# Pooled attention and a chosen expert: choosing the expert, loading its weights, the first tiles' keys and the rows set aside, rearranged

## The chip, the cores and the metric

The kernel runs on one core of one Trainium2 chip. The number that counts is the device time of one execution in microseconds (us). The engines have short names here: PE multiplies matrices, DVE works on vectors, ACT applies functions, POOL is GpSimd, SP only issues transfers (DMAs). Each engine runs its own list of instructions strictly in order and waits where an input isn't there yet.

## The reference

```python
kv_pool = kv.reshape(B, H // 4, 4, W // 4, 4, C).mean(axis=(2, 4))
k = v = kv_pool.reshape(B, -1, C) @ w_sr              # 768 keys a batch
a = softmax(q @ k.T / sqrt(C));  x = (a @ v).reshape(B * S, D)
logits = x @ w_gate;  expert_idx = argmax(logits)      # 8 experts
out[row] = softmax(logits)[expert] * (relu(x[row] @ w1[expert]) @ w2[expert])
```

There are 4 batches of 12288 queries with 128 channels, 768 pooled keys for each batch, 8 experts with 1024 hidden features. All is float32.

## The kernel before

The queries are cut into 96 tiles of 512 rows, 24 to a batch (`SPB`). A tile goes through attention (scores of 768 keys, maximum, exponential, transposes, values), the gate's logits, the routing, and the expert's two layers. Each float32 product is made of three matmuls on a high and a low part of the operands (`mm3`, lines 221 to 223): `kh`/`kl`, `qh`/`ql`, `pth`/`pt`, `xh`/`xl`, `hh`/`hlow`, `wt`. ACT makes the high parts (line 215), DVE or POOL the low ones (lines 218 and 909).

In a batch nearly all rows choose the same expert. `pick` finds it from the first tile of a batch: it marks each row's expert (`oh`, line 533), adds the marks (`tot`), lets PE sum them over the 128 partitions (line 546), and takes the largest. SP reads its number into a register and loads the two weight matrices (`load_weights`); `cut` splits them into a high part (ACT) and a low part (POOL, 4 pieces). The first layer is `first()`, the second `second()`; every tile is computed with its batch's expert.

Rows with another expert are strangers. When a chunk of tiles has been routed (three chunks in a batch: tiles 0 to 8, 9 to 16, 17 to 23), `collect` ranks its strangers (`xoh`, `bt`, `xtot`, a sum on PE in lines 637 and 638, then `pos` on POOL and `place`) and `put_row` (line 689) writes them with one indirect DMA of POOL for each 128 rows into `lists`, 4 units of time apart. The last batch's rows are put only at the end of the program and only if need be. Two extra tiles (`EXTRA`), inserted in the last batch, take 128 rows of `lists` each (line 1008, `xid`), gather their queries and compute them. After the last tile DVE counts what is left (`more`, lines 1201 to 1207); every engine loads `more` (line 1208) and, if it is not zero, runs a loop over the rest. In the run shown it is zero.

The keys of a batch are averaged on DVE (`raw`, line 264), turned on PE, projected (line 306) and split. For batch 0 this happens at the start; for the others during the batch before. The first three tiles (`FIRST`) transpose their exponentials on PE (line 808), and write them in the keys' interleaved order; all later ones transpose on DVE and DMA.

The order on each engine follows from a plan: a heap of (time, function). `AT` is a table of offsets for a tile's steps in units (16 units to a tile, one tile takes about 20 us). `plan.at` places a step, `series` a chain of steps that waits for a free bank of PSUM. What is popped first is emitted first, and engines run it in that order. Three PSUM banks are handed round with `take` and `give`.

Of the kernel before, what the change touches and what calls it, by code (L numbers as in the profile page):

```python
# [30 lines left out]
    "turn_q": -17.69, "high_q": -9.56, "low_q": -7.35, "maxima": 1.36, "exps": 1.9, ("scores", 0): 0.0,  # L31
    ("scores", 1): 3.8, ("scores", 2): 8.16, ("scores", 3): 12.21, ("first_p", 0): 8.67, ("first_p", 1): 5.16,
    ("first_p", 2): 4.44, ("first_p", 3): 8.51, ("first_p", 4): 5.05, ("first_p", 5): 5.87, "first_high": 0.8,
    "first_low": 1.23, "first_values": 2.54, "turn_p": 3.06, "move_p": 17.26, ("high_p", 0): 23.35,
    ("high_p", 1): 26.36, ("high_p", 2): 28.89, "low_p": 6.59, ("values", 0): 34.89, ("values", 1): 37.47,
    ("values", 2): 37.48, ("values", 3): 40.72, ("values", 4): 45.71, ("values", 5): 46.95, "high_x": 0.7,
    "low_x": 1.18, "logits": 3.5, "diag": 4.81, "route": 6.37, "step": 0.4, "scale_exp": 2.53, "scale": 3.11,
    "apart": 5.66, "spread": 7.89, "keep_s": 8.68, ("first", 0): 66.38, ("first", 1): 67.88,
    ("first", 2): 68.9, ("first", 3): 70.58, ("first", 4): 73.63, ("first", 5): 74.3, ("first", 6): 76.79,
    ("first", 7): 78.4, "high_h": 0.57, "low_h": 1.51, "second": 5.06, "turn_y": 0.94, "scale_y": 2.2,  # L40
    "put": 9.84, "early_q": -13.19, "cut": -3.88, "cut_step": 1.05,
# [39 lines left out]
def tile_pooled_attention_top1_moe(ctx: ExitStack, tc, q, kv, w_sr, w_gate, w1, w2, out):  # L81
# [68 lines left out]
    eidx = iota("eidx", [[1, E]], 0, 0)  # L150
    order_l = iota("order_l", [[-1, NL]], NL, 0)
# [91 lines left out]

    def keys(t, b, step):
# [66 lines left out]
        def high_kv(kb):  # L311
            pr, ks = own["pr", kb], slice(kb * P, (kb + 1) * P)
            nc.scalar.mul(out=own["kh"][:, ks], in_=pr[:, :P], mul=scale)
            high(own["vh"][:, kb], pr[:, P : P + C])

        def low_kv(kb):
# [13 lines left out]
        for kb in range(NB):  # L330
# [17 lines left out]
    def load_weights(own):  # L348
        for n in range(2):
            own[n] = kp.tile([P, POOL // 2, POOL * C], F32, name="raw", bufs=3)  # L350
        nc.sync.dma_start(
            out=own[0].rearrange("p r c -> p (r c)"),
            in_=w1[bass.ds(own["ex"], 1)].rearrange("o p f -> p (o f)"),
        )
        nc.sync.dma_start(
            out=own[1].rearrange("p r (f d) -> p (r f) d", d=D),
            in_=w2[bass.ds(own["ex"], 1)].rearrange("o (f p) d -> p (o f) d", p=P),
        )
# [18 lines left out]
    chunks = [range(0, 9), range(9, 17), range(17, SPB)]  # L377
# [15 lines left out]
    def route(t, i, own):  # L393
# [44 lines left out]
        def firsts():  # L438
# [4 lines left out]
            )  # L443

# [150 lines left out]
    def collect(t, b, c):  # L595
# [88 lines left out]
        if b < B - 1:  # L684
            steps += [(4.0 if n else 1.0, put_row, b, c, n) for n in range(A)]
# [556 lines left out]
```

## Time and profile before

| | us |
|---|---|
| median of 3 runs | 2071.72 (2071.35 to 2072.4) |
| profiled execution | 2071.68 |
| its span in the profile | 2070.0 |
| PE busy | 2008.7 (97%) |
| DVE busy | 1605.3 (78%) |
| ACT busy | 1323.6 (64%) |
| POOL busy | 1317.9 (64%) |

The span is the time from the first to the last event of the profile, and 1.7 us of the execution lie outside it. A busy share is an average over the whole span. A wait is told by the engine that waited, what ended it, and how long the engine had been idle. The start of an operation and its length stand in the timeline; when two operations overlap in an engine's pipeline, their lengths add up to slightly more than the time they take.

### The profile page before, as it was taken

The numbers are of one execution on the slowest core, as the hardware profiler recorded it, in microseconds if no ns is written. First come the engines' busy times: TensorE is split into PE (matmuls) and PEld (weight loads), VectorE is DVE, ScalarE is ACT, GpSimd is POOL, SyncE is SP. The second block draws the span as 40 slices with busy tenths as digits, with TensorE's granted clock in tenths as the row PEclk, the third lists the DMA queues.
The fourth block names the chain that finished last, engine by engine and source line by source line (L and its number), as shares of the span: only waits on it lengthen the run. The fifth ranks groups of instructions, "written<-read, shape, count | busy, mean of one in ns | idle before, by whom it ended". The sixth has DMA issues, their size and how long they took to land.

```text
span 2070.0 us, 29923 instructions
## 1 busy us (share of the span) xinstructions
PE 2008.7 (97%) x9358; PEld 1657.5 (80%) x9358; DVE 1605.3 (78%) x2646; ACT 1323.6 (64%) x2630; POOL 1317.9 (64%) x1163
## 2 busy tenths in 40 slices
PE   6899999999999999999999999999999999999997
PEld 5688888878878888878878888887887888887885
DVE  5677779987777788997787777998777777777764
ACT  3666666666666666666666666666666666666663
POOL 1154576687687666777778657668678765545441
PEclk9899999999999999999999999999999999999998
DMA  6455556655565455756456545665646454646431
GB/s 172 74 122 114 105 100 147 149 122 115 113 131 119 96 119 107 151 124 141 95 126 129 118 91 119 129 146 126 127 91 131 92 119 95 161 83 143 97 77 22
DMA packets 497652, 239.91 MB, mean 116 GB/s; under 512 B 427440, under 2 KB 433714, under 8 KB 497488
## 3 DMA queue, kind: packets, MB, share of 16 engines
q1 hardware_dynamic: 488144, 237.69, 54.8%
q0 software_dynamic: 9344, 0.26, 0.3%
q8 instruction: 75, 1.23, 0.2%
q14 instruction: 89, 0.73, 0.1%
HBM read 59.97 MB, written 31.92 MB: 44 GB/s over the span
## 4 chain that ended last, share of the span: by engine, by line
PE 87%; DVE 6%; DMA 2%; SPq 1%; issue 1%; ACT 1%; POOL 1%; DVEq 0%; POOLq 0%; ACTq 0%
PE ps L221 28%; PE ps L223 28%; PE ps L222 28%; DVE hlow L909 1%; DVE nmax L751 1%; PE ps L403 1%; PE ps L402 1%; DVE pb L778 1%; SPq L788 1%; ACT prob L768 1%; DVE half L264 1%; PE ps L306 0%; PE ps L808 0%; SPq L258 0%; DMA pt<-pb 0%
## 5 line engine op out<-in xcount | busy, mean ns | idle before, releaser
L909 DVE SCALAR_TENSOR_TENSOR hlow<-ps,hh 128x512 fp32r<-128x512 f32 x768 | 520.1, 678 | 225.7 <-ACT hh L905 214.7
L218 POOL TENSOR_TENSOR pt<-pt,pth 128x1024 fp32r<-128x1024 f32 x279 | 672.9, 2415 | 34.0 <-ACT pth L215 26.8
L905 ACT ACTIVATE hh<-ps 128x512 fp32r<-128x512 f32 x768 | 458.6, 597 | 328.4 <-PE ps L223 224.5
L768 ACT ACTIVATE prob<-ps,nmax 128x768 f32<-128x768 f32 x384 | 354.4, 923 | 272.6 <-DVE nmax L751 259.4
L778 DVE STREAM_TRANSPOSE pb<-prob 128x768 f32<-128x768 f32 x372 | 359.0, 965 | 107.0 <-ACT prob L768 104.8
L751 DVE TENSOR_REDUCE nmax<-ps 128x1 f32<-128x768 f32 x384 | 363.5, 947 | 57.3 <-PE ps L223 49.5
L689 POOL DMA_INDIRECT lists<-row,dst x288 | 289.2, 1004 | 60.6 <-issue 54.8
L221 PE MATMUL ps<-hh,wt 128*128 128x512 f32 x768 | 312.0, 406 | 0.0
L221 PE MATMUL ps<-xh,wt 128*128 128x512 f32 x768 | 306.5, 399 | 2.7 <-ACT wt L215 2.5
L223 PE MATMUL ps<-xl,wt 128*128 128x512 f32 x768 | 305.5, 398 | 0.0
L222 PE MATMUL ps<-xh,wt 128*128 128x512 f32 x768 | 304.2, 396 | 0.6 <-POOL wt L218 0.6
L222 PE MATMUL ps<-hh,wt 128*128 128x512 f32 x768 | 303.2, 395 | 0.0
L223 PE MATMUL ps<-hlow,wt 128*128 128x512 f32 x768 | 303.1, 395 | 0.0
L215 ACT CAST pth<-pt 128x1024 fp32r<-128x1024 f32 x279 | 291.8, 1046 | 16.0 <-DMA pt<-pb 14.6
L221 PE MATMUL ps<-kh,qh 128*128 128x256 f32 (+2 forms) x768 | 260.9, 340 | 3.3 <-ACT prob L768 3.1
L223 PE MATMUL ps<-kl,qh 128*128 128x256 f32 (+2 forms) x768 | 260.1, 339 | 0.0
L222 PE MATMUL ps<-kh,ql 128*128 128x256 f32 (+2 forms) x768 | 260.0, 339 | 0.0
L937 POOL TENSOR_TENSOR yo<-yb,sb 128x512 f32<-128x512 f32 x96 | 101.0, 1052 | 221.6 <-issue 109.3
L223 PE MATMUL ps<-pt,vh 128*128 128x512 f32 x558 | 220.7, 396 | 0.0
L221 PE MATMUL ps<-pth,vh 128*128 128x512 f32 x558 | 220.6, 395 | 0.0
L222 PE MATMUL ps<-pth,vl 128*128 128x512 f32 x558 | 218.5, 392 | 0.0
L218 POOL TENSOR_TENSOR ql<-qt,qh 128x512 fp32r<-128x512 f32 x96 | 125.0, 1302 | 117.1 <-ACT qh L215 62.2
(212 smaller groups left out, 2987.5 us busy)
## 6 DMA issues: line engine op xcount, KB each, us to landing
pt<-pb SPq DMA_DIRECT2D x372, 384.0 KB
qb<-in_q_dram SPq DMA_DIRECT2D x384, 64.0 KB
out_dram<-yo SPq DMA_DIRECT2D x384, 64.0 KB
raw<-in_kv_dram SPq DMA_DIRECT2D x84, 256.0 KB
raw<-in_moe_w_dram SPq DMA_DIRECT2D x12, 512.0 KB
lists<-row,dst POOLq DMA_INDIRECT x288, 2.3
pth<-in_kv_dram SPq DMA_DIRECT2D x12, 256.0 KB
kvs<-kh SPq DMA_DIRECT2D x4, 384.0 KB
```

The costliest lines, as they stand in the source:

```text
L215: nc.scalar.copy(out=dst, in_=src)
L218: eng.tensor_tensor(out=dst, in0=src, in1=h.bitcast(F32), op=ALU.subtract)
L221: nc.tensor.matmul(out=ps, lhsT=wh, rhs=xh, start=start, stop=False)
L222: nc.tensor.matmul(out=ps, lhsT=wl, rhs=xh, start=False, stop=False)
L223: nc.tensor.matmul(out=ps, lhsT=wh, rhs=xl, start=False, stop=stop)
L689: put = nc.gpsimd.indirect_dma_start(out=lists, out_offset=bass.IndirectOffsetOnAxis(ap=state["dst", b, c][:, n : n + 1].bitcast(U32), axi ...
L751: nc.vector.tensor_reduce(out=nmax, in_=own["s", a], op=ALU.max, axis=AX.XY if i < HEAD else AX.X, negate=True)
L768: nc.scalar.activation(out=p_out, in_=s_in, func=AF.Exp, bias=own["nmax", a], scale=1.0, accum_out=grp["sums"][:, k : k + 1],)
L778: nc.vector.transpose(out=own["pb"][:, :, :, a, :].rearrange("p c b t -> p b c t"), in_=own["prob", a].rearrange("p (b c t) -> p b c t", c ...
L905: nc.scalar.activation(out=hh, in_=own["hp", f], func=AF.Relu)
L909: nc.vector.scalar_tensor_tensor(out=hl, in0=own["hp", f], scalar=0.0, in1=own["hh", f].bitcast(F32), op0=ALU.max, op1=ALU.subtract,)
L937: nc.gpsimd.tensor_tensor(out=own["yo"], in0=own["yb"].rearrange("p (n d) -> p n d", d=SQ), in1=sb.unsqueeze(2).broadcast_to([P, G * G, SQ ...
```

## The change

`pick` loses `oh`: the routing's own marks `sc` (8 for expert 0 down to 1) are added at once, and the sums weighed with `even`. Weights come in four DMAs, two for each matrix, and `first()` and `second()` wait each for their own piece. The chunks become four (0 to 8, 9 to 16, 17 to 20, 21 to 23). In the last batch the rows of the first three chunks are put during the batch, 2 units apart, and `more` is made in the last chunk's `collect`. The first three tiles write their exponentials contiguously: batch 0's keys are in natural order for them, with own value tiles `v_first` (in the spare weight buffer), and a second projection makes the interleaved values (`values_project`). The last tile is computed in two halves of 256 columns, turned and scaled by DVE, and written from two queues. The extra tiles wait for a free bank, and their `turn_q` comes later. The table `AT` has new numbers.

```diff
-    "put": 9.84, "early_q": -13.19, "cut": -3.88, "cut_step": 1.05,
+    "second": 5.06, "turn_y": 0.58, "scale_y": 2.2, "put": 9.84, "early_q": -13.17, ("cut", 0): -3.88,
+    ("cut", 1): -0.27, ("cut", 2): 0.9, ("cut", 3): 1.28, "values_first": 0.3, "extra": -0.18,
+    "extra_q": 14.55, "count": 0.96, "ranks": 0.61,
...
+    v_first = [wts[1][:, n, : NB * C].rearrange("p (n c) -> p n c", c=C) for n in range(2)]
...
+        def mean_first(kb):
+            own["pTn", kb] = kp.tile([P, P], F32, name="pooled")
+            nc.scalar.mul(out=own["pTn", kb], in_=own["pt", kb][:, :P], mul=1.0 / (POOL * POOL))
+            give(own["pt", kb])
+            own["pT", kb] = kp.tile([P, P], F32, name="pooledT")
+            nc.gpsimd.tensor_copy(out=by_key(own["pT", kb]), in_=split_keys(own["pTn", kb]))
...
+            if b == 0:
+                nc.tensor.matmul(out=pr[:, :P], lhsT=wsr_sb, rhs=own["pTn", kb], start=True, stop=True)
+                nc.tensor.matmul(out=pr[:, P : P + C], lhsT=own["pTn", kb], rhs=wsr_sb, start=True, stop=True)
+                return
...
+        @takes_bank
+        def values_project(kb):
+            own["pv", kb] = take()
+            nc.tensor.matmul(out=own["pv", kb][:, :C], lhsT=own["pT", kb], rhs=wsr_sb, start=True, stop=True)
...
-        nc.sync.dma_start(
-            out=own[0].rearrange("p r c -> p (r c)"),
-            in_=w1[bass.ds(own["ex"], 1)].rearrange("o p f -> p (o f)"),
-        )
...
+        for c in range(F // T):
+            cs = slice(c * T, (c + 1) * T)
+            nc.sync.dma_start(
+                out=own[0][:, c], in_=w1[bass.ds(own["ex"], 1), :, cs].rearrange("o p f -> p (o f)")
+            )
...
-    chunks = [range(0, 9), range(9, 17), range(17, SPB)]
+    chunks = [range(0, 9), range(9, 17), range(17, 21), range(21, SPB)]
...
-        def onehot():
-            after("first", b, 0)
-            own["oh"] = rp.tile([P, G, E], F32, name="oh")
...
+                nc.vector.reduce_sum(
+                    out=own["tot"], in_=state["group", b, 0]["sc"].rearrange("p g e -> p e g"), axis=AX.X
+                )
...
+            own["av"] = own["ct"][:, E : 2 * E]
+            nc.vector.tensor_tensor(out=own["av"], in0=own["ct"][:, :E], in1=even, op=ALU.mult)
...
+            if b == B - 1:
+                steps += [(0.1, counts, n) for n in range(3)]
+        if b < B - 1 or c < len(chunks) - 1:
+            step = 4.0 if b < B - 1 else 2.0
+            steps += [(step if n else 1.0, put_row, b, c, n) for n in range(A)]
...
-            if i < FIRST:
-                p_out = by_key(prob).rearrange("p (h n) c t -> p h n c t", h=2)
-                s_in = s_in.rearrange("p h (n c t) -> p h n c t", t=SQ, c=P // SQ)
-            elif i < HEAD:
+            if i < HEAD:
                 p_out = prob.rearrange("p (h k) -> p h k", h=2)
...
-            for n in range(2):
-                for c in range(F // T):
-                    after("cut", b, n, c)
+            after("cut", b, 0, f * P // T)
...
+        def last_y(h):
...
+            nc.vector.transpose(out=own["yb"][:, hs], in_=own["y"][h])
+            nc.vector.tensor_tensor(
+                out=own["yo"][:, ts], in0=own["yb"][:, hs].rearrange("p (n d) -> p n d", d=SQ),
...
+                (nc.sync if k % P < 2 * SQ else nc.scalar).dma_start(
...
-        t += 8.0
+        t += AT["extra_q"]
...
-    go = nc.values_load(more[0:1, 0:1], min_val=0, max_val=NTOK // P + NL)
+    go = nc.values_load(state["more"][0:1, 0:1], min_val=0, max_val=NTOK // P + NL)
     with tc.If(go > 0):
-        for c, tiles in enumerate(chunks):
-            for n in range(len(tiles) * G):
-                put_row(B - 1, c, n)
+        for n in range(len(chunks[-1]) * G):
+            put_row(B - 1, len(chunks) - 1, n)
```

On POOL, where the second batch begins, the program before runs these steps from the end of the first batch's last `collect` (`left`) to the first low part of the second batch's weights (`wt_78`); `lists` are the puts.

```order
L674 TENSOR_TENSOR left<-rows,start 128x8
L937 TENSOR_TENSOR yo<-yb,sb 128x512
L689 DMA lists<-row,dst 397312x2 x2
L459 TENSOR_TENSOR dn<-df,rinv 128x32
L218 TENSOR_TENSOR ql<-qt,qh 128x512
L689 DMA lists<-row,dst 397312x2 x2
L218 TENSOR_TENSOR pt<-pt,pth 128x4x256
L486 TENSOR_TENSOR sx<-row,quad 128x16
L689 DMA lists<-row,dst 397312x2
L218 TENSOR_TENSOR wt_78<-raw,wt_78 128x512
```

After the change the same stretch of POOL reads:

```order
L710 TENSOR_TENSOR left<-rows,start 128x8
L1004 TENSOR_TENSOR yo<-yb,sb 128x512
L743 DMA lists<-row,dst 397312x2 x3
L502 TENSOR_TENSOR dn<-df,rinv 128x32
L226 TENSOR_TENSOR ql<-qt,qh 128x512
L743 DMA lists<-row,dst 397312x2 x3
L226 TENSOR_TENSOR pt<-pt,pth 128x4x256
L529 TENSOR_TENSOR sx<-row,quad 128x16
L743 DMA lists<-row,dst 397312x2 x2
L226 TENSOR_TENSOR wt_78<-raw,wt_78 128x512
```

Eight puts stand there in place of five; in the whole stretch from the `dn` two tiles earlier there are 22 in place of 12.

On DVE, at the ranks of the second chunk's strangers, the program before has these steps up to `xtot`, the operand of PE's sum:

```order
L712 STREAM_TRANSPOSE qt<-qb 128x4x4x32
L778 STREAM_TRANSPOSE pb<-prob 128x6x4x32
L625 TENSOR_REDUCE bt<-xoh 128x64
L909 SCALAR_TENSOR_TENSOR hlow<-ps,hh 128x512
L632 TENSOR_REDUCE xtot<-bt 128x8
L218 TENSOR_TENSOR xl<-ps,xh 128x512
```

After the change they read:

```order
L962 SCALAR_TENSOR_TENSOR hlow<-ps,hh 128x512
L829 STREAM_TRANSPOSE pb<-prob 128x6x4x32
L661 TENSOR_REDUCE bt<-xoh 128x64
L668 TENSOR_REDUCE xtot<-bt 128x8
L962 SCALAR_TENSOR_TENSOR hlow<-ps,hh 128x512
L226 TENSOR_TENSOR xl<-ps,xh 128x512
```

One `hlow` that stood ahead of `xtot` stands behind it.

On DVE at the end of the program before, `more` is the last thing that is made:

```order
L665 TENSOR_REDUCE place<-pos 128x28
L909 SCALAR_TENSOR_TENSOR hlow<-ps,hh 128x512 x7
L932 STREAM_TRANSPOSE yb<-ps 128x512
L1201 TENSOR_SCALAR cnt<-left 128x32
L1202 TENSOR_SCALAR cnt<-cnt 128x32
L1207 TENSOR_REDUCE more<-cnt 128x1
```

After the change the end of DVE's list reads:

```order
L701 TENSOR_REDUCE place<-pos 128x12
L718 TENSOR_SCALAR cnt<-left 128x32
L720 TENSOR_SCALAR cnt<-cnt 128x32
L727 TENSOR_REDUCE more<-cnt 128x1
L962 SCALAR_TENSOR_TENSOR hlow<-ps,hh 128x512 x7
L1015 STREAM_TRANSPOSE yb<-ps 128x256
L1016 TENSOR_TENSOR yo<-yb,sb 128x256
L1015 STREAM_TRANSPOSE yb<-ps 128x256
L1016 TENSOR_TENSOR yo<-yb,sb 128x256
```

The three steps that make `more` have moved ahead of seven `hlow` and of the last tile's result, and the last product stands on DVE.

## Rows read from the trace of the kernel before

**Rows 1.** The page, busy time of the engines: us (share of the span) xinstructions.

```profile
PE 2008.7 (97%) x9358; PEld 1657.5 (80%) x9358; DVE 1605.3 (78%) x2646; ACT 1323.6 (64%) x2630; POOL 1317.9 (64%) x1163
```

**Rows 2.** The waits of PE over the whole span. A line of the program that waited, what it waited for: us in total, times, longest us.

```profile
PE ps L546 <- DVE tot L541: 7.0, 3, 2.4
PE ps L637 <- DVE xtot L632: 6.2, 4, 1.9
PE ps L808 <- ACT prob L768: 5.6, 4, 2.4
...
PE ps L221 <- ACT prob L768: 3.1, 4, 1.8
...
PE ps L1034 <- DVE hlow L909: 1.7, 1, 1.7
...
PE ps L1034 <- DMA half<-in_q_dram,xidn: 1.3, 1, 1.3
```

**Rows 3.** The end of the program. First the timeline (start us, us, engine line op out<-in, idle time before it and what ended it), then what lines 1208, 1209 and 1238 issued there (engine's queue, operation, times, shortest/median/longest ns, first and last start in us).

```profile
2047.13 0.20 POOL L674 TENSOR_TENSOR left<-rows,start 128x8 f32<-128x8 f32 x1
...
2054.88 0.40 PE L223 MATMUL ps<-hlow,wt 128*128 128x512 f32 x1
...
2055.38 0.72 DVE L932 STREAM_TRANSPOSE yb<-ps 128x512 f32<-128x512 f32 x1 [1.07 <-PE ps L223]
...
2056.23 1.05 POOL L937 TENSOR_TENSOR yo<-yb,sb 128x512 f32<-128x512 f32 x1 [7.89 <-issue]
...
2057.31 2.75 SPq L946 DMA_DIRECT2D out_dram<-yo  x4
...
L1208 POOLq TENSOR_LOAD <-more x1: 513/513/513, 2056.6 to 2056.6; - x1
...
L1209 POOLq EVENT_SEMAPHORE  x5: 17/43/43, 2060.2 to 2060.6; - x5
...
L1209 POOLq INC_SWDGE_SEM  x1: 1795/1795/1795, 2060.7 to 2060.7; - x1
...
L1238 POOLq DRAIN  x3: 40/107/6615, 2062.5 to 2069.7; - x3
...
L1238 SPq DRAIN  x3: 7/7/13, 2063.2 to 2069.4; - x3
```

**Rows 4.** The timeline of ACT, an exponential of the first tile and one of the fourth.

```profile
36.69 1.60 ACT L768 ACTIVATE prob<-ps,nmax 128x768 f32<-128x768 f32 x1 [2.02 <-DVE nmax L751]
...
90.45 0.90 ACT L768 ACTIVATE prob<-ps,nmax 128x768 f32<-128x768 f32 x1 [1.68 <-DVE nmax L751]
```

**Rows 5.** What line 306 issued: the projection of the pooled keys on PE, shortest/median/longest ns, first and last start.

```profile
L306 PE MATMUL ps<-pooledT,wsr_sb x48: 386/406/582, 13.3 to 1435.0; 128*128 128x128 f32 x48
```

**Rows 6.** One stretch of the span: from:to, length, busy us (instructions) of PE, PE's weight loads, DVE, ACT and POOL, granted clock of PE as a share of full speed, DMA share, GB/s.

```profile
50.00:100.00 50.00, 40.13 (x185) 32.80 (x184) 32.15 (x64) 31.49 (x65) 8.92 (x10) 0.88 0.43 75
```

**Rows 7.** The timeline of PE where batch 1's expert is chosen: the count of `tot`, and the first `first()` that uses batch 1's weights.

```profile
575.16 0.17 PE L546 MATMUL ps<-tot,ones 128*128 128x8 bf16 x1 [2.29 <-DVE tot L541]
...
586.78 0.40 PE L221 MATMUL ps<-xh,wt 128*128 128x512 f32 x1
587.02 0.39 PE L222 MATMUL ps<-xh,wt 128*128 128x512 f32 x1
```

**Rows 8.** The timeline of DVE at the same place.

```profile
572.81 0.18 DVE L446 TENSOR_REDUCE chosen<-sc 128x4 f32<-128x32 f32 x1
573.02 1.84 DVE L533 TENSOR_TENSOR oh<-chosen,order 128x32 f32<-128x32 f32 x1
```

**Rows 9.** The timeline of POOL at the same place.

```profile
573.52 1.28 POOL L218 TENSOR_TENSOR ql<-qt,qh 128x512 fp32r<-128x512 f32 x1
...
583.68 1.28 POOL L218 TENSOR_TENSOR wt<-raw,wt 128x512 fp32r<-128x512 f32 x1 [1.19 <-ACT wt L215]
```

**Rows 10.** Two stretches of 2 us behind that wait, columns as in rows 6.

```profile
576.00:578.00 2.00, 2.00 (x6) 1.61 (x5) 1.08 (x5) 2.00 (x5) 1.69 (x2) 0.50 0.02 1
578.00:580.00 2.00, 2.00 (x7) 1.52 (x7) 2.00 (x5) 1.70 (x3) 1.67 (x1) 0.66 0.66 201
```

**Rows 11.** POOL in the 54.48 us from the `dn` at 530.48 to the end of the first low part of batch 1's weights: first the stretch (busy us (instructions), clock, DMA share, GB/s), then its costliest groups (busy us, mean ns of one | idle before, releasers).

```profile
530.48:584.96 54.48, 41.78 (x46) 0.97 0.49 103
...
L218 POOL TENSOR_TENSOR pt<-pt,pth 128x1024 fp32r<-128x1024 f32 x7 | 16.9, 2418 | 0.1
L689 POOL DMA_INDIRECT lists<-row,dst x12 | 12.1, 1011 | 3.4 <-issue 2.5 <-DMA raw<-in_moe_w_dram 0.5 <-DMA out_dram<-yo 0.3
L218 POOL TENSOR_TENSOR ql<-qt,qh 128x512 fp32r<-128x512 f32 x3 | 3.9, 1290 | 0.0
L937 POOL TENSOR_TENSOR yo<-yb,sb 128x512 f32<-128x512 f32 x2 | 2.1, 1046 | 1.6 <-DMA pt<-pb 1.6
L218 POOL TENSOR_TENSOR wt<-raw,wt 128x512 fp32r<-128x512 f32 x1 | 1.3, 1282 | 1.2 <-ACT wt L215 1.2
```

**Rows 12.** The timeline of DVE before PE's first wait for the ranks of strangers.

```profile
418.63 0.68 DVE L909 SCALAR_TENSOR_TENSOR hlow<-ps,hh 128x512 fp32r<-128x512 f32 x1
419.22 0.26 DVE L632 TENSOR_REDUCE xtot<-bt 128x8 bf16<-128x64 f32 x1
```

**Rows 13.** The timeline of POOL at the first extra tile.

```profile
1766.06 0.19 POOL L1023 CAST xidn<-xid 128x1 int32<-128x1 f32 x1 [4.42 <-DMA xid<-lists]
```

**Rows 14.** What line 689 issued: the puts, shortest/median/longest ns, first and last start.

```profile
L689 POOL DMA_INDIRECT lists<-row,dst x288: 966/1005/1297, 262.0 to 1695.0; - x144
```

More of the change, by code (lines that the diff above doesn't have):

```diff
@@ L36 @@
[L36 to L40, printed above, removed]
@@ L548, in weigh @@
         def weigh():
-            own["av"] = rp.tile([P, E], F32, name="av")
-            nc.vector.scalar_tensor_tensor(
-                out=own["av"], in0=own["ct"][:, :E], scalar=2.0 * E, in1=order, op0=ALU.mult, op1=ALU.add
-            )
-            give(own["ct"])
+            own["av"] = own["ct"][:, E : 2 * E]
+            nc.vector.tensor_tensor(out=own["av"], in0=own["ct"][:, :E], in1=even, op=ALU.mult)
         def top():
@@ L574, in others @@
             )
+            give(own["ct"])
         def fetch():
@@ L676, in counted, with counts @@
             )
+        def counts(n):
+            if n == 0:
+                state["cnt"] = rp.tile([P, NL], I32, name="cnt", bufs=1)
+                nc.vector.tensor_scalar(out=state["cnt"], in0=left, scalar1=float(P - 1), scalar2=None, op0=ALU.add)
+            elif n == 1:
+                nc.vector.tensor_scalar(
+                    out=state["cnt"], in0=state["cnt"], scalar1=int(math.log2(P)), scalar2=None,
+                    op0=ALU.arith_shift_right,
+                )
+            else:
+                state["more"] = rp.tile([P, 1], I32, name="more", bufs=1)
+                with nc.allow_low_precision("small whole numbers"):
+                    nc.vector.reduce_sum(out=state["more"], in_=state["cnt"], axis=AX.X)
         steps = [
-            (0, number), (0.6, onehot), (0.6, strangers), (0.6, by_tile), (0.6, totals), (0.6, ranks), (0.3, places),
+            (0, number), (0.6, onehot), (0.6, strangers), (0.6, by_tile), (0.6, totals), (AT["ranks"], ranks), (0.3, places),
             (0.6, before), (2, own_place), (1, place), (1, whole),
@@ L921, in second @@
             done("second", i, f)
+            after("cut", b, 1, f * P // T)
             fs = slice(f * D, (f + 1) * D)
+            if i == NS - 1:
+                own["y"] = [ps[:, k, : T // 2] for k in (BANK_Y, 1)]
+                for y, h in zip(own["y"], range(0, T, T // 2)):
+                    hs = slice(h, h + T // 2)
+                    mm3(
+                        y, wt[:, 2, fs], wt[:, 3, fs], own["hh", f][:, hs], own["hl", f][:, hs],
+                        f == 0, f == FB - 1,
+                    )
+                return
             mm3(
@@ L1115, in split_h, with result @@
             give(own["hp", n])
+        @takes_bank
+        def result():
+            own["yp"] = take()
         def second(n):
-            if n == 0:
-                own["yp"] = take()
             for k in range(G):
@@ L1183, in extra @@
         at(t + 4, put)
+        todo.sort(key=lambda step: step[0])
+        steps.series(t0, [(u - w, *rest) for (u, *rest), (w, *_) in zip(todo, [(0.0,)] + todo)], lambda: len(free) > 1)
     keys(-54, 0, 6)
```

129 lines of the change are left out of this document (83 added, 46 removed).

## The prediction

> **What bounds the kernel now.** I read the page's busy shares first, then the waits of PE, then PE in stretches of time, and only then the other engines in the stretches where PE waited. The reader should see that PE is busy for 2008.7 of 2070.0 us [rows 1]: this kernel is a queue of matmuls, and an engine beside it matters only where PE stands still. The waits of PE that the change touches come in four places [rows 2]: the first 100 us (L808 and L221 behind the exponentials), the choice of a batch's expert (L546, 7.0 us in three), the ranks of strangers (L637, 6.2 in four), and the two extra tiles (L1034, 1.7 and 1.3). A fifth place is no wait of PE: its last matmul begins at 2054.88 and the span ends at 2070.0 [rows 3]. The table of times moves work within a tile, but the count of matmuls per tile stays, so I put the new table at nothing in the tiles where PE is full; what it could cost there is bounded by the stalls of a tile, which [rows 2] do not show in the middle of a batch. It may lose 0.05 us a tile, 5 us over 96 tiles, or gain nothing.
>
> **The tail.** In before DVE turns the last tile (0.72 us), only then makes `more`, POOL scales (2056.23, 1.05 us), and SP issues four writes (2.75 us, to 2060.06). POOL, PE, ACT and DVE load `more` at 2056.6; POOL then jumps, clears its queue's semaphores (from 2060.7, 1.795 us) and sits in a drain from 2062.5 for 6.615 us to 2069.1, after all the others [rows 3]. So POOL's chain, 2070.0 − 2056.6 = 13.4 us from its load of `more`, ends last, not the output. After, `more` is made by the last collect, whose last POOL step ends at 2047.3 in before [rows 3]; three DVE operations of about 0.2 us later, near 2048, POOL can load it, and its chain would end at 2061.4. The output is then as late: last matmul ends 2055.3, two turns and two products on DVE (0.36 each, half of 0.72, and about 0.5, half of POOL's 1.05) to 2057.0, two issues of 0.69 on each of two queues to 2058.4 against 2060.06, so 1.7 us less than before; SP's part behind it took from 2060.06 to 2063.2 (its own drain) and would end near 2061.5, plus 0.9 for the last barrier: 2062.4. The tail gives **−8**. From both sides: −2 if POOL's drain waits for the output's writes, −9 if the output costs nothing.
>
> **The head.** The exponentials of the first three tiles write in the keys' order and take 1.60 us, the fourth tile's 0.90 [rows 4]; the change makes twelve of them like the fourth: 0.70 each. PE waited for them seven times before 100 us, 5.6 + 2.9 us [rows 2]. At one exponential per wait that is 4.9; less what is added ahead of the first scores. There stand six more matmuls of a 128x128 f32 operand (0.4 us each [rows 5]) with a cast and a difference each; PE is idle in most of that time, so only the last block's, about 0.4, is in the path. The extra copies by POOL lie beside it, POOL being busy 8.9 of 50 us there [rows 6]. The granted clock is 0.88 between 50 and 100 us [rows 6]: of 40 busy us some 5 go to the lower level; shorter gaps give back perhaps 1.5. Sum −4.9 + 0.4 − 1.5 = **−6**; bounds −1 (the next operation, a maximum on DVE, is late instead) and −10 (all 8.5 and the clock).
>
> **The choice of the expert.** PE reaches the count at 575.16 − 2.29 = 572.87 and waits for `tot`, because `oh` ran from 573.02 for 1.84 us [rows 7, 8]. `oh` reads two operands from SBUF and ends with POOL's `ql` (573.52 + 1.28) [rows 8, 9]. The Trainium skill (SBUF — State Buffer, section "SBUF: two separate sides") says that a VectorE operation with two SBUF inputs and a GpSimd operation lock each other out; the trace agrees, 1.84 us here. After, `oh` is gone and the sum follows `chosen` (0.18 us), so `tot` is ready near 573.3: a wait of 0.4 in place of 2.29. The clock after this stall was 0.50 and 0.66 for 2 us each [rows 10], which is 2 × 0.50 + 2 × 0.34 = 1.7 us. So the next batch's first `first()` could start 1.9 + 1.7 = 3.6 us sooner than at 586.78 [rows 7], at 583.2.
>
> What is late next is the weights' low part on POOL. Its second matmul, 587.02 in before, needs the first piece of `wt`, which POOL began at 583.68 [rows 9]. In the order of after, from the `dn` at 530.48 to that piece, POOL has 22 puts in place of 12, since a batch's chunks now overlap: pairs where single puts stood, then three. The work: seven `pt` 16.9, three `ql` 3.9, two `yo` 2.1, the piece 1.3, and 21 small operations that took the remaining 5.5 of the stretch's 41.8 busy us [rows 11] and are fewer and 3 tiles wide in place of 7, so about 4.0; and 22 × (1.011 + 0.21 of issue, 2.5 us over twelve [rows 11]) = 26.9. That is 55.1 us of work without a hole: 585.6. The holes that remain, at least two waits for DVE, bring it to about 586.0. So PE waits at the second matmul of `first()` until 586.0: 1.0 us ahead of before's 587.02, not 3.6. This wait is about 2.5 us long, as long as the one that dropped the clock, and I charge the same 1.7 us behind it. Per batch −1.0 + 1.7 = +0.7, three times **+2**. From both sides: −10.8 if POOL never makes PE wait (3 × 3.6), +20 if puts are slow (the rival below). Four pieces of the weights in place of two move the same bytes and let `first()` wait for one piece; it costs nothing as long as POOL is the later one.
>
> **Ranks.** `xtot` stands behind an `hlow` of 0.68 us in before [rows 12] and ahead of it in after, with the same place on PE; three times 0.6, less a bit that the `hlow` is late, is **−1.5** (bounds −8: all of 6.2 and a clock drop; +6: the fourth collect brings three waits of 1.9 more).
>
> **Extra tiles.** Later `turn_q` and the readiness of banks can take both L1034 waits, 3.0 us [rows 2]. Against this, in the last batch 84 puts are now issued at eight a tile, 9.8 us of POOL in each 20-us tile, and POOL stands still for `xid` until 1766.06 [rows 13] with puts and splits behind it. I put 2 us of waiting there: **−1** (bounds −3 to +6).
>
> **Sum.** −8 − 6 + 2 − 1.5 − 1 = −14.5. The profiled execution took 2071.68 us (span 2070.0 and 1.7 around it), and the median is 2071.72, so the forecast is 2071.7 − 14.5 = 2057.2, said as **2057**.
>
> **The rivals.** (a) *POOL keeps up and the choice's wait goes for good.* For it: in before POOL was busy for 41.8 of 54.5 us in that stretch, so it isn't full by nature. Against it: the 22 puts are counted, not guessed. Time: 2071.7 − 8 − 6 − 10.8 − 1.5 − 1 = 2044.4. Chance 0.25.
>
> (b) *The end of the program stays behind the output.* POOL's drain would wait for the last writes; for it speaks that POOL's next recorded step after its load of `more` at 2056.6 came at 2060.2 [rows 3], when SP's issues also ended. Tail −2, time 2063. Chance 0.12.
>
> (c) *Slower: the puts choke POOL.* A put took 0.966 to 1.297 us [rows 14]. At 1.297 + 0.21 each the 22 puts cost 6.3 us more, and PE's first matmul of each batch waits that much longer: 3 × 6.3 = 19, and 2 or 3 more in the last batch, against −14.5: 2071.7 + 7 = 2079. It decides from 0.22 us more per put (14.5 / 3 / 22). The same page of the Trainium skill, same section, warns that GpSimd cannot write descriptors while VectorE holds the shared port. The rows bear this out little: the median put took 1.005 [rows 14] with DVE busy 78% of the span [rows 1]. Chance 0.13.
>
> The forecast itself has 0.50, with its own range of 2051 to 2064.
>
> **How the numbers follow.** A measurement of this kernel can tell about 0.2%, 4 us: faster means under 2067.6. Of the cases, (a), nearly all of the forecast's and most of (b) are under it: 0.25 + 0.48 + 0.10 = 0.83. Same: 0.07, from the rest of (b) and mild (c). Slower: 0.10. For eight times in ten the range reaches from the near half of (a), 2043, to 2070, which leaves out most of (c) and the better end of (a), with the table's 5 us inside.
>
> **What would show it.** Tail: last matmul to span end under 8 us in place of 15. Head: exponentials of 0.9 us from the start, and PE busy above 42 in 50 to 100 us. Choice: L585's wait under 1 us three times, and in its place waits of 2 to 4 us of the second matmul of `first()` on POOL's `wt`; if that line doesn't appear, (a) holds. Ranks: L673 near 4 us. Wrong altogether if new waits stand in the middle of batches (a `pt`, `ql` or `hlow` in every tile), where 0.15 us per tile would undo the gain.

## The result and the profile after

The changed kernel takes 2088.63 us (median of 4 runs, 2086.53 to 2092.13), the kernel before in the same comparison 2072.06 us. The ratio is 1.0081 with a 95% interval of 1.0063 to 1.0098: it is slower by some 16.6 us, where 14.5 us less were forecast. The profiled execution took 2092.13 us with a span of 2090.4, so it is 3.5 us above the median; the places below are read from it.

Where the time went is read by putting the two timelines side by side: the start of the first full-width score matmul (`kh,qh`, 512 columns) of a tile, in before and in after.

| tile | before, us | after, us | after minus before |
|---|---|---|---|
| 4 | 91.50 | 86.73 | -4.77 |
| 16 | 332.28 | 328.68 | -3.60 |
| 27 | 560.49 | 560.30 | -0.19 |
| 29 | 604.96 | 609.71 | +4.75 |
| 51 | 1055.07 | 1061.64 | +6.57 |
| 53 | 1099.65 | 1109.75 | +10.10 |
| 75 | 1549.70 | 1561.65 | +11.95 |
| 77 | 1594.22 | 1608.51 | +14.29 |
| 85 | 1754.64 | 1769.68 | +15.04 |
| 95 | 1977.89 | 2000.48 | +22.59 |
| last matmul | 2054.88 | 2082.91 | +28.03 |
| end of the span | 2070.0 | 2090.4 | +20.4 |

So the head gained 4.8 us and the tail 7.6, and everything between lost. Four losses can be told apart: a jump where a new batch's expert is chosen (tiles 27 to 29, 51 to 53, 75 to 77), a jump in the last batch, a little at the ranks, and a slow drift of 0.1 us per tile in all tiles. The drift is the one that no wait shows. In the middle of the second batch no matmul waits in either kernel, and these rows stand ten tiles apart, first in before:

```profile
624.91 0.39 PE L221 MATMUL ps<-kh,qh 128*128 128x512 f32 x1
...
825.41 0.39 PE L221 MATMUL ps<-kh,qh 128*128 128x512 f32 x1
```

and in after:

```profile
629.74 0.39 PE L229 MATMUL ps<-kh,qh 128*128 128x512 f32 x1
...
831.18 0.39 PE L229 MATMUL ps<-kh,qh 128*128 128x512 f32 x1
```

A tile takes 20.050 us before and 20.144 after. Over the 92 tiles from tile 4 on that is 8.7 us. A tile has 92 matmuls, so one takes 1 ns more in the mean.

The waits of PE after (line, what it waited for: us in total, times, longest us), which answer to [rows 2]:

```profile
PE ps L673 <- DVE xtot L668: 8.7, 6, 1.5
PE ps L230 <- POOL wt L226: 7.5, 4, 2.3
PE ps L229 <- DVE hlow L962: 5.8, 6, 2.1
PE ps L859 <- ACT prob L819: 4.8, 3, 1.8
...
PE ps L229 <- ACT prob L819: 4.3, 7, 1.3
PE ps L536 <- POOL sx L529: 3.7, 4, 1.2
PE ps L231 <- POOL pt L226: 3.1, 3, 1.3
```

The wait for `tot`, 7.0 us in [rows 2], is gone at two of the three choices; at the third the same line, L585, waits 1.5 us behind DVE's `rinv`. In its place stand L230 behind POOL's `wt`, L536 behind POOL's `sx` and L231 behind POOL's `pt`: three lines that did not wait on POOL in the middle of the run before. The six waits of L673 on `xtot` are 1.41 us three times, at the second chunk, and 1.50 us three times, at the third. In before the ranks waited four times. At the second batch the timeline of PE reads so:

```profile
563.19 0.17 PE L673 MATMUL ps<-xtot,upper 128*128 128x8 bf16 x1 [1.50 <-DVE xtot L668]
...
584.97 0.40 PE L536 MATMUL ps<-sx,sel 128*128 128x16 f32 x2 [1.16 <-POOL sx L529]
...
586.00 0.39 PE L229 MATMUL ps<-xh,wt 128*128 128x512 f32 x1
...
588.72 0.80 PE L230 MATMUL ps<-xh,wt 128*128 128x512 f32 x1 [2.32 <-POOL wt L226]
```

`first()` reaches its second matmul and waits 2.3 us until POOL has made the weights' low part; the same stands at 1090.18 and 1590.00. Behind it the granted clock drops (stretches of 2 us: busy us (instructions) of PE, its weight loads, DVE, ACT and POOL, then the clock, DMA share, GB/s):

```profile
588.00:590.00 2.00, 1.28 (x3) 1.10 (x4) 0.00 (x0) 0.00 (x0) 1.81 (x3) 0.53 0.82 222
590.00:592.00 2.00, 2.00 (x6) 1.54 (x6) 0.69 (x1) 1.62 (x3) 2.00 (x1) 0.50 0.93 177
592.00:594.00 2.00, 2.00 (x6) 1.54 (x5) 0.61 (x1) 1.03 (x4) 1.83 (x3) 0.50 0.76 153
594.00:596.00 2.00, 2.00 (x10) 1.73 (x9) 0.88 (x2) 0.03 (x1) 1.58 (x2) 0.77 0.18 26
...
1090.00:1092.00 2.00, 1.82 (x4) 1.49 (x5) 0.00 (x0) 0.50 (x2) 1.81 (x3) 0.50 0.88 192
1092.00:1094.00 2.00, 2.00 (x7) 1.56 (x6) 0.69 (x1) 1.59 (x5) 2.00 (x2) 0.68 0.90 194
...
1590.00:1592.00 2.00, 2.00 (x9) 1.64 (x10) 0.54 (x1) 1.17 (x3) 1.87 (x2) 1.00 0.79 216
```

At the lower of its two levels (1.2 in place of 2.4 GHz) from 590 to 594, and partly before and after, PE loses 0.6 of its 1.28 busy us, then 1.0, 1.0 and 0.5: 3.1 us, against 1.7 in [rows 10]. At the third batch the loss is 1.6 us. At the fourth, behind a wait just as long, the clock doesn't fall.

POOL's work from the `dn` to the end of the first piece of `wt`, 530.58 to 588.67, which answers to [rows 11] (busy us, mean ns of one | idle before, releasers):

```profile
L743 POOL DMA_INDIRECT lists<-row,dst x22 | 21.8, 993 | 6.2 <-issue 5.5 <-PE ps L585 0.3 <-DMA out_dram<-yo 0.2
L226 POOL TENSOR_TENSOR pt<-pt,pth 128x1024 fp32r<-128x1024 f32 x7 | 16.9, 2410 | 0.0
L226 POOL TENSOR_TENSOR ql<-qt,qh 128x512 fp32r<-128x512 f32 x3 | 3.9, 1312 | 0.0
L1004 POOL TENSOR_TENSOR yo<-yb,sb 128x512 f32<-128x512 f32 x2 | 2.1, 1051 | 0.0
L226 POOL TENSOR_TENSOR wt<-raw,wt 128x512 fp32r<-128x512 f32 x1 | 1.3, 1286 | 0.0
```

The 22 puts are there, and the stretch takes 58.1 us in place of the forecast 55.5 (530.48 to 586.0). Beside the gaps before the puts, POOL stands still twice, for a `row` of DVE:

```profile
537.85 0.39 POOL L529 TENSOR_TENSOR sx<-row,quad 128x16 f32<-128x16 f32 x2 [0.83 <-DVE row L520]
...
559.09 0.22 POOL L529 TENSOR_TENSOR sx<-row,quad 128x16 f32<-128x16 f32 x1 [0.79 <-DVE row L520]
```

The end of the program in the timeline after, which answers to [rows 3]:

```profile
2082.91 0.28 PE L231 MATMUL ps<-hlow,wt 128*128 128x256 f32 x1
...
2084.25 0.43 DVE L1016 TENSOR_TENSOR yo<-yb,sb 128x256 f32<-128x256 f32 x1
...
2083.88 2.83 SPq L1023 DMA_DIRECT2D out_dram<-yo  x4
...
2083.89 2.88 ACTq L1023 DMA_DIRECT2D out_dram<-yo  x4
```

and POOL's queue there (times, shortest/median/longest ns, first and last start):

```profile
L1302 POOLq TENSOR_LOAD <-more x1: 597/597/597, 2074.5 to 2074.5; - x1
...
L1331 POOLq DRAIN  x3: 40/107/4816, 2077.5 to 2090.2; - x3
```

POOL loads `more` 8.4 us ahead of the last matmul and has finished its drain at 2082.3 (2077.5 + 4.8), before the last product. What ends last is now the output on the queues of SP and ACT.

### The profile page after: what moved, and what is told of

It reads as the page before. It is cut to its first block, busy times and chain, and to the rows that moved or that the text cites. A ratio compares the mean times of both kernels' runs of the same rounds, so it can differ in the third digit from the quotient of the medians.

```text
span 2090.4 us, 30313 instructions
## 1 busy us (share of the span) xinstructions
PE 2020.0 (97%) x9402; PEld 1654.6 (79%) x9402; DVE 1645.1 (79%) x2677; ACT 1319.7 (63%) x2636; POOL 1404.4 (67%) x1276
## 5 line engine op out<-in xcount | busy, mean ns | idle before, releaser
L819 ACT ACTIVATE prob<-ps,nmax 128x768 f32<-128x768 f32 x384 | 346.1, 901 | 296.8 <-DVE nmax L805 284.8
L743 POOL DMA_INDIRECT lists<-row,dst x372 | 370.8, 997 | 85.2 <-issue 76.7
L229 PE MATMUL ps<-xh,wt 128*128 128x512 f32 x768 | 306.3, 399 | 8.5 <-DVE hlow L962 5.6
L230 PE MATMUL ps<-xh,wt 128*128 128x512 f32 x768 | 305.6, 398 | 7.6 <-POOL wt L226 7.5
L229 PE MATMUL ps<-hh,wt 128*128 128x512 f32 (+1 forms) x776 | 312.4, 403 | 0.0
L230 PE MATMUL ps<-hh,wt 128*128 128x512 f32 (+1 forms) x776 | 306.5, 395 | 0.0
L231 PE MATMUL ps<-hlow,wt 128*128 128x512 f32 (+1 forms) x776 | 305.8, 394 | 0.0
L231 PE MATMUL ps<-xl,wt 128*128 128x512 f32 x768 | 304.7, 397 | 0.0
L229 PE MATMUL ps<-kh,qh 128*128 128x256 f32 (+2 forms) x768 | 261.8, 341 | 4.7 <-ACT prob L819 4.3
L230 PE MATMUL ps<-kh,ql 128*128 128x256 f32 (+2 forms) x768 | 260.4, 339 | 0.0
L231 PE MATMUL ps<-kl,qh 128*128 128x256 f32 (+2 forms) x768 | 259.1, 337 | 0.0
L231 PE MATMUL ps<-pt,vh 128*128 128x512 f32 x558 | 220.4, 395 | 3.1 <-POOL pt L226 3.1
L229 PE MATMUL ps<-pth,vh 128*128 128x512 f32 x558 | 222.2, 398 | 0.0
L230 PE MATMUL ps<-pth,vl 128*128 128x512 f32 x558 | 222.2, 398 | 0.0
```

The source lines that it names most:

```text
L229: nc.tensor.matmul(out=ps, lhsT=wh, rhs=xh, start=start, stop=False)
L230: nc.tensor.matmul(out=ps, lhsT=wl, rhs=xh, start=False, stop=False)
L231: nc.tensor.matmul(out=ps, lhsT=wh, rhs=xl, start=False, stop=stop)
L743: put = nc.gpsimd.indirect_dma_start(out=lists, out_offset=bass.IndirectOffsetOnAxis(ap=state["dst", b, c][:, n : n + 1].bitcast(U32), axi ...
L819: nc.scalar.activation(out=p_out, in_=s_in, func=AF.Exp, bias=own["nmax", a], scale=1.0, accum_out=grp["sums"][:, k : k + 1],)
```

## The experiments

**The table.** The first run takes the old numbers back, for every step that both kernels have (the first lines of the table, as they stand in the two kernels).

```diff
-    "turn_q": -18.01, "high_q": -9.56, "low_q": -7.35, "maxima": 1.27, "exps": 1.9, ("scores", 0): 0.0,
-    ("scores", 1): 4.2, ("scores", 2): 7.73, ("scores", 3): 12.21, ("first_p", 0): 8.9, ("first_p", 1): 4.44,
...
+    "turn_q": -17.69, "high_q": -9.56, "low_q": -7.35, "maxima": 1.36, "exps": 1.9, ("scores", 0): 0.0,
+    ("scores", 1): 3.8, ("scores", 2): 8.16, ("scores", 3): 12.21, ("first_p", 0): 8.67, ("first_p", 1): 5.16,
...
```

> The changed kernel with the numbers of the table AT of the kernel before, for every step that both have (the new keys keep their new numbers). Theory A (the new table makes every tile 0.09 us longer, 92 tiles): 2088.6 - 8.5 = about 2080, and the scores of consecutive tiles stand 20.05 us apart in the middle of a batch. Rival B (the 0.09 us belong to the execution or the chip, not to the table): about 2088, tiles 20.14 us apart, or the kernel before shows the same 20.14 on this chip.

It took 2086.25 us (2084.83 to 2087.52), ratio to before 1.0066 [1.0047, 1.0085], and its tiles stand 20.121 us apart (626.31 to 827.52 for ten). So the table has 0.023 us of the 0.094 us a tile. The time is 2.4 us less, with ranges that overlap. Theory A falls, for the greater part of the drift is elsewhere. Rival B was put wrong too: the pace of 20.144 came back to the ns in the profiles of the next two runs, so it belongs to the program and not to an execution.

**The puts of the last batch.** The second run leaves them to the branch at the end.

```diff
-        if b < B - 1 or c < len(chunks) - 1:
-            step = 4.0 if b < B - 1 else 2.0
+        if b < B - 1:
+            step = 4.0
...
-        for n in range(len(chunks[-1]) * G):
-            put_row(B - 1, len(chunks) - 1, n)
+        for c, tiles in enumerate(chunks):
+            for n in range(len(tiles) * G):
+                put_row(B - 1, c, n)
```

> The changed kernel, but no rows of the last batch are put during the batch (all 96 puts stand in the branch at the end that isn't taken). Theory A (POOL is choked by the puts in the last batch): the waits of L231 and L536 on POOL after 1790 us and the waits of L229 on hlow go, 9 us less: about 2079. Rival B (the order of the steps in the last batch costs it, not the puts): 2086 to 2089.

2082.52 us (2078.07 to 2086.10), ratio 1.0056 [1.0035, 1.0077]: 6.1 us less, not 9, and the four executions lie 8 us apart. The waits of L231 on `pt` are gone from the list of waits, L536 waits once (1.2); L229 still waits 3.5 us for `hlow` in three places. Theory A holds, and its size is open between two readings: the medians give 6 us, and by place, from tile 85 to the last matmul, the loss against before falls from 13.0 to 3.0 us, which is 10.

**The chunks.** The third run goes back to three chunks besides.

```diff
-    chunks = [range(0, 9), range(9, 17), range(17, 21), range(21, SPB)]
+    chunks = [range(0, 9), range(9, 17), range(17, SPB)]
```

> As the run before, and the chunks are three again (0 to 8, 9 to 16, 17 to 23). Theory A (the fourth chunk's ranks, 1.5 us three times, and its puts, which delay sx and the first piece of the weights at each new batch, cost the batch changes): another 12 us less, about 2067, with no wait of L230 on wt. Rival B (the weights come late whatever the chunks, since the pick now ends sooner): L230 still waits some 2 us three times, and the time is 2074 or more.

2063.73 us (2060.84 to 2068.07), ratio 0.9962 [0.9949, 0.9975]: 18.8 us less than the run before, more than theory A said. L230 waits 0.6 us once, in the first 100 us, and L673 three times in place of six. Without early puts, the fourth chunk alone makes the difference between a gain and a loss.

**The addresses.** What is left of the drift sits in matmuls that wait for nothing. From start to start, over ten tiles of the third batch, a matmul with `hh` as the moving operand took 234.9 ns in before and 236.9 in after, one with `hlow` 231.2 and 233.8, one that uses `vl` 229.2 and 234.7 (sums of the differences of starts in the timeline, divided by their number). One with `xh` and `wt` took 232.2 and 232.1. The change adds one constant tile, `even`, of 32 bytes a partition. In the program's memory map the large tiles behind it (keys, queries, exponentials, `x` and hidden features) start 32 bytes past a multiple of 64, where before they start at multiples of 256: `hh` at 196384 in place of 196352, `pth` at 95008 in place of 94976. Two runs were made on it. In one the changed kernel gets a wider tile:

```diff
-    even = cp.tile([P, E], F32, name="even")
+    even = cp.tile([P, 2 * E], F32, name="even")[:, :E]
```

> The changed kernel, with the small tile `even` allocated 64 bytes wide and not 32, so that every tile behind it in SBUF starts at a multiple of 64 bytes, as in the kernel before. Theory A (operands that start at 32 past a multiple of 64 bytes make PE's matmuls some ns longer): consecutive tiles 20.07 us apart in place of 20.146, 92 x 0.07 = 6.5 us less, about 2082. Rival B (the addresses don't matter; waits do): 2088 and 20.146.

2084.81 us (2082.58 to 2089.99), ratio 1.0058 [1.0041, 1.0076]; tiles 20.117 us apart (627.72 to 828.89). The pace moved, by 0.027 us a tile and not by 0.07: multiples of 64 bytes are not what it takes. In the other the kernel before gets the tile:

```diff
+    even = cp.tile([P, E], F32, name="even")
+    nc.vector.reciprocal(out=even, in_=order)
     order_l = iota("order_l", [[-1, NL]], NL, 0)
```

> The kernel before with one more tile of 32 bytes among the constants (and one reciprocal that fills it), which moves every later tile by 32 bytes. Theory A: tiles 20.12 us apart in place of 20.05, 6.5 us more, about 2078.5. Rival B: 2072 and 20.05.

2078.40 us (2075.70 to 2080.98), ratio 1.0030 [1.0021, 1.0040]. The same two rows in its trace:

```profile
629.79 0.39 PE L223 MATMUL ps<-kh,qh 128*128 128x512 f32 x1
...
831.00 0.39 PE L223 MATMUL ps<-kh,qh 128*128 128x512 f32 x1
```

20.121 us a tile, with not one matmul more or another order: 32 bytes in the constants and the `reciprocal` that fills them cost the kernel before 6.4 us. This is theory A's figure; a run below has the same `reciprocal` without the shift.

**The two together.** Three chunks, no early puts and the tile of 64 bytes:

```diff
-    chunks = [range(0, 9), range(9, 17), range(17, 21), range(21, SPB)]
+    chunks = [range(0, 9), range(9, 17), range(17, SPB)]
...
+    even = cp.tile([P, 2 * E], F32, name="even")[:, :E]
```

> Three chunks, no puts of the last batch before the end, and the 64-byte `even`. Theory A: 2063.7 - 6.5 = about 2057, tiles 20.07 us apart. Rival B: 2063.7.

2061.09 us (2059.60 to 2062.36), ratio 0.9940 [0.9923, 0.9956], tiles at 20.117 us: 2.6 us less than with 32 bytes (3.8 less with four chunks), and short of the 6.5.

**Puts further apart.** Is it the fourth chunk or its puts? This run keeps four chunks and the early puts of the last batch, with the 64-byte tile, and spreads the puts of the third and fourth chunk over twice the time.

```diff
-            step = 4.0 if b < B - 1 else 2.0
+            step = (8.0 if c > 1 else 4.0) if b < B - 1 else 2.0
```

> The changed kernel with the 64-byte `even`, and the puts of the third and fourth chunk of the first three batches 8 units apart in place of 4, so that fewer stand ahead of a batch's first weights on POOL. Theory A (those puts make the weights and sx late): the waits of L230 on wt (2.3 us three times) and of L536 on sx go at the batch changes, about 12 us less than with the 64-byte `even` alone, near 2070; the wait of L673 on the third chunk's xtot (1.5) stays. Rival B (the weights are late by the loads): L230 still waits 2 us three times.

2066.33 us (2064.96 to 2068.38), ratio 0.9966 [0.9954, 0.9979]: 18.5 us less than with the 64-byte tile alone. The waits of PE:

```profile
PE ps L673 <- DVE xtot L668: 4.6, 4, 1.4
PE ps L231 <- POOL pt L226: 3.2, 3, 1.3
PE ps L536 <- POOL sx L529: 1.7, 2, 1.2
PE ps L230 <- POOL wt L226: 1.6, 4, 0.6
```

L230 waits at most 0.6 us. L673 fell from 9.1 us with the 64-byte tile alone to 4.6, which theory A had not expected: the 1.5 us before the third chunk's `xtot` were POOL's too, since `bt`, from which it is made, needs an `xoh` that POOL makes behind the puts. With one number of the plan changed, each change of batch went from a loss to a gain: from tile 27 to 29 the distance to before moves by -3.2 us, with the 64-byte tile alone by +4.5.

**Where the tiles start at multiples of 256 bytes.** `even` becomes 256 bytes wide, with three chunks and no early puts.

```diff
+    even = cp.tile([P, 8 * E], F32, name="even")[:, :E]
```

> Three chunks, no puts of the last batch before the end, and `even` allocated 256 bytes wide, so that all later tiles start at multiples of 256 bytes as in the kernel before. Theory A (the start address within 256 bytes sets PE's pace): tiles 20.07 us apart (20.05 and the new table's 0.024), 92 x 0.045 = 4 us less than with 64 bytes: about 2057. Rival B (the pace comes from the change's other instructions; 64 bytes was as good as it gets): 2061 and 20.117.

2056.77 us (2055.28 to 2058.24), ratio 0.9932 [0.9916, 0.9949]: the fastest version that was run, 14.4 us below the kernel before in its comparison. Ten tiles:

```profile
617.12 0.39 PE L229 MATMUL ps<-kh,qh 128*128 128x512 f32 x1
...
817.79 0.39 PE L229 MATMUL ps<-kh,qh 128*128 128x512 f32 x1
```

20.067 us, before's 20.050 and the table's share. And the kernel before with the same tile:

```diff
+    even = cp.tile([P, 8 * E], F32, name="even")[:, :E]
+    nc.vector.reciprocal(out=even, in_=order)
```

> The kernel before with a constant tile of 256 bytes more (and the reciprocal that fills it). Theory A: 2072, tiles 20.05 us apart, since all addresses keep their place within 256 bytes. Rival B (any move of the tiles, or the extra instruction, costs it): 2076 to 2079, tiles 20.09 to 20.12 apart.

2071.35 us (2069.45 to 2072.94) against 2071.17, ratio 0.9999 [0.9989, 1.0009], tiles at 20.050 (624.79 to 825.29). Neither the reciprocal nor the move as such costs anything. The pace follows the start address of the large tiles: 20.05 at multiples of 256, 20.12 at 32 past. Through which access it does so is open. With the shift alone the matmuls on `hh`, `hlow` and `vl` became longer, as above (236.7, 232.9 and 233.3 ns), and those on `xh` and `wt` did not (232.1), though `xh` moved by the same 32 bytes. The transfers became longer too: the packets of the main queue (q1), as many and as many bytes, took 56.8% of the 16 DMA engines' span with the shift, against 54.8% in before and 55.1% with 256 bytes. Whether PE's own operands do it, moving or stationary, or the transfers beside them, was not tried.

**Early puts alone.** As the version of 2056.77, with the first two chunks of the last batch put early:

```diff
-        if b < B - 1:
-            step = 4.0
+        if b < B - 1 or c < len(chunks) - 1:
+            step = 4.0 if b < B - 1 else 2.0
```

> As e8, but the first two chunks of the last batch are put during the batch, 2 units apart, as in the change. Theory A (eight puts a tile choke POOL at the extra tiles): waits on sx, pt and hlow return after 1780 us, 4 to 6 us more than e8, about 2062. Rival B (only the fourth chunk's puts on top of them did harm): as e8.

2061.40 us (2060.17 to 2063.52), ratio 0.9958 [0.9941, 0.9975]. The time is what theory A said, 4.6 us more. The places aren't: in the profile this run reaches tile 4 at 86.39 us and the other at 83.46, 2.9 us of the difference before any put, in a stretch where the programs have the same work: PE waited 6.9 us there for averaged keys (L296 behind DVE's `pth`) and in the other 3.3. Only 0.9 us come later (last matmul at 2050.73 and 2046.91), and one wait of L231 on `pt`, 0.8 us, is new. The time is inconclusive. At most about 1.7 us belong to the puts, and from tile 85 to the last matmul 0.5: by place, rival B is nearer.

**The old mark.** As the version of 2056.77, with the expert picked by `oh`:

```diff
+        def onehot():
+            after("first", b, 0)
+            own["oh"] = rp.tile([P, G, E], F32, name="oh")
...
-                    out=own["tot"], in_=state["group", b, 0]["sc"].rearrange("p g e -> p e g"), axis=AX.X
+                    out=own["tot"], in_=own["oh"].rearrange("p g e -> p e g"), axis=AX.X
...
-            nc.vector.tensor_tensor(out=own["av"], in0=own["ct"][:, :E], in1=even, op=ALU.mult)
+            nc.vector.scalar_tensor_tensor(
+                out=own["av"], in0=own["ct"][:, :E], scalar=2.0 * E, in1=order, op0=ALU.mult, op1=ALU.add
+            )
```

> As e8, but the expert is picked as before (oh, totals of oh, weighed with order). Theory A (oh's lock with POOL costs 1.9 us and the clock behind it 1.7, three times): L585 waits 2.3 us three times, about 9 to 11 us more than e8: 2066 to 2068. Rival B (the wait only moves to the weights): within 2 us of e8.

2062.60 us (2061.32 to 2063.88), ratio 0.9960 [0.9946, 0.9974]. In the profile `oh` stands again between `chosen` and `tot`, in the timeline of DVE:

```profile
571.15 1.57 DVE L577 TENSOR_TENSOR oh<-chosen,order 128x32 f32<-128x32 f32 x1
572.75 0.21 DVE L585 TENSOR_REDUCE tot<-oh 128x8 bf16<-128x32 f32 x1
```

PE waits for `tot` twice, 2.3 us each:

```profile
PE ps L592 <- DVE tot L585: 4.6, 2, 2.3
```

Without `oh`, in the version of 2056.77, the sum follows at once:

```profile
567.90 0.17 DVE L489 TENSOR_REDUCE chosen<-sc 128x4 f32<-128x32 f32 x1
568.00 0.19 DVE L578 TENSOR_REDUCE tot<-sc 128x8 bf16<-128x32 f32 x1
```

From tile 27 to 29 this run keeps step with before (+0.05), the other gains 2.6; the same at tile 75, and nothing separates them at tile 51. 5.3 us in two places: theory A, smaller than its 9 to 11. This run too begins 2.9 us later than the one it is compared with.

**Closing the sum.** The change as it is, only with the 256-byte tile:

```diff
-    even = cp.tile([P, E], F32, name="even")
+    even = cp.tile([P, 8 * E], F32, name="even")[:, :E]
```

> The change as it is, with four chunks and early puts, only `even` allocated 256 bytes wide. It closes the sum: the addresses' share of the change is this run against 2088.6, the chunks' and puts' share this run against e8's 2056.8. Theory A: the addresses gave 0.07 us a tile, 6.5 us: about 2082, tiles 20.07 us apart. Rival B (in the full change PE's waits on POOL absorb it, since POOL sets the pace at the batch changes): 2086 or more.

2080.84 us (2077.69 to 2082.64), ratio 1.0045 [1.0028, 1.0061]; tiles 20.068 apart (622.25 to 822.93). The addresses have 7.8 us of the change; against 2056.77 the fourth chunk and the early puts have 24.1 us. By place, early puts cost the last batch little with three chunks and much with four: from tile 85 to the last matmul the loss against before is 4.9 us without them, 5.5 with them and three chunks, 10.5 here. That the version of 2056.77 meets the forecast of 2057 is chance, since its parts do not: the head gains 8.0 us there and not 6, the three choices gain 9.3 where 2 were to be lost, and the last batch loses 4.9 where 1 was to be won.

## Why the prediction was wrong

| term | forecast, us | by place in the profiles, us |
|---|---|---|
| tail | -8 | -7.6 |
| head | -6 | -4.8 |
| choice of the expert, three times | +2 | +10.2 |
| ranks | -1.5 | +1.9 |
| extra tiles, last batch | -1 | +11.9 |
| table, all tiles | 0 | +8.7 |
| sum | -14.5 | +20.3 |

The right column is from the table of the first section, with 0.095 us a tile taken off each stretch and gathered in the last line; the ranks are the rest of the stretches between tile 4 and tile 85 (tiles 16 to 21 above all); the third chunk's `xtot` falls into the row of the choice. The last batch is tile 85 to the last matmul, and the sum stands against a span longer by 20.4.

**The tail was right, by another end.** The size, 7.6 for 8, came out. POOL's drain took 4.8 and not 6.6 us and was over before the last product, which rules out rival (b); the output ends last, and it issues four writes on each queue, 2.83 us, where I had two.

**The head came near in size, in part by luck.** The exponentials take 0.9 us, and the first tiles end 4.8 us earlier. PE's waits for them fell from 8.5 [rows 2] to 6.0 us in the first 100 us: 2.5 won where 4.9 were said. The clock rose from 0.88 to 0.93 between 50 and 100 us as forecast, but in the first 50 it fell from 0.97 to 0.86, which no term had. Over the profiles of the changed kernels the gain at tile 4 runs from 4.6 to 8.0 us; in part this is the wait for averaged keys, as shown above, and what moves it between programs with the same work there was not found.

**The choice of the expert failed in its price: of POOL's queue only one wait was charged.** The wait itself came where the forecast had it: L230 waits 2.3 us three times where 2.5 was said. But PE reaches that matmul at 586.4 (588.72 less the wait) and not at 583.5, and POOL's piece is ready at 588.7 and not at 586.0. PE is late because the same queue holds `sx` (L536, 1.2 us) and, through `xoh`, the third chunk's `xtot` (1.5 us). The sum had neither; the bound of the ranks' term had named the second. POOL is late by 2.6 us: the two waits for `row` came to 1.6 us where 0.4 was allowed for holes. The 22 puts with their gaps took 28.0 and not 26.9, since the second put of a pair stands 0.30 behind the first and the gaps came to 0.28 a put, not 0.21. The small operations took 4.5 and not 4.0. And the clock behind the waits cost 3.1, 1.6 and 0 us at the three choices, where 1.7 was said for each. So the forecast of +0.7 a batch was +4.8, +3.3 and +2.1. Rival (a), that POOL keeps up, is what the runs with three chunks and with slower puts show: -2.6 to -4.0 a change where -3.6 was said.

**Rival (c) named the place and missed the price.** The puts did choke POOL, but a put took 0.993 us in the mean, no more than in [rows 14]; the count and the order of the 22 were enough, without any slower put. The warning of the Trainium skill (SBUF — State Buffer, section "SBUF: two separate sides") that GpSimd can't write descriptors while VectorE holds the port is not seen here: the mean is 993 ns with DVE busy 79% of the span. How long DVE held that port was not counted.

**The last batch failed too:** it was put at a loss of 2 us against a gain of 3, and by place it lost 11.9. Eight puts a tile were priced in POOL's time, and of the waits that they bring only 2 us were allowed; without the early puts some 6 to 10 us of the loss go. The two waits of L1034 did go, and in their place stand waits on `pt`, `sx` and `hlow`:

```profile
1823.51 0.50 PE L231 MATMUL ps<-pt,vh 128*128 128x512 f32 x1 [0.82 <-POOL pt L226]
...
1923.58 0.51 PE L229 MATMUL ps<-xh,wt 128*128 128x512 f32 x1 [1.21 <-DVE hlow L962]
...
1928.05 0.51 PE L229 MATMUL ps<-xh,wt 128*128 128x512 f32 x1 [2.12 <-DVE hlow L962]
...
2040.09 0.50 PE L231 MATMUL ps<-pt,vh 128*128 128x512 f32 x1 [0.97 <-POOL pt L226]
...
2044.92 0.51 PE L231 MATMUL ps<-pt,vh 128*128 128x512 f32 x1 [1.30 <-POOL pt L226]
```

Ahead of the two at 2040 the third chunk's puts begin, four in a row from 2032.74 to 2037.63, right behind the second chunk's last at 2030.22; no step of the forecast had that. The waits on `hlow` stay without any early puts (two of 2.1 us in the version of 2056.77), so other steps make them; which was not found.

**The ranks** kept most of their wait: `xtot` ahead of `hlow` gave 1.4 in place of 1.9 us, three times. The loss in this row is the first batch's, 2.4 us. There a wait of 0.57 us for `prob` stood right ahead of the 1.41, and the clock fell behind them (0.50 from 418 to 420 us, 0.79 to 422), some 1.5 us; in before it stayed at 1.00 behind the 1.88. In the next two batches before lost clock here (0.50 from 914 to 916 and from 1410 to 1412 us) and after did not, and after won 0.2 us each. Which of such waits the clock answers was not forecast and was not found.

**The table was put at nothing, for the wrong reason.** The sentence "the count of matmuls per tile stays, so I put the new table at nothing in the tiles where PE is full" took a full PE for a constant pace. The drift is 8.7 us where the sum had 0: the new order costs 0.02 us a tile, and 32 bytes of constants cost 0.07. The 5 us allowed for it held the table and not the addresses.

## What to carry to other kernels

Where a queue of one engine feeds several waits, sum its work up to each deadline with the gaps between its instructions, and ask of every instruction behind the late one who waits for it; here one number of the plan, puts 8 units apart and not 4, was worth 18.5 us. When a kernel is bound by matmuls, compare the pace of a stretch in which nothing waits before reading any wait, and when it moved, look at where the large tiles start in SBUF. Keep small constants from moving them: rounding the new one up to 256 bytes gave the pace back here.

## What was not expected of the hardware

PE's pace depends on where the large tiles start in SBUF: ten tiles of the same matmuls in the same order take 200.5 us when the large tiles start at multiples of 256 bytes and 201.2 us when they start 32 bytes later, 6.4 us in the kernel's time. At 64 past a multiple of 256 the changed kernel lay between, 20.117 against 20.067 and 20.144 us a tile.

The end of POOL's queue is no fixed price: its drain took 6.6 us before and 4.8 after, the clearing of its semaphores 1.8 and 1.3 us.
